# A hand-written plan that takes in the SyncE queue: the last loads of v, the first expert's weights and the end of the attention stage in another order

## The chip, the core and the metric

The kernel runs on one core of a Trainium2 chip. Five engines work side by side, each through its own list of instructions in order: TensorE (PE: matrix products and transposes), VectorE (DVE), ScalarE (ACT), GpSimd (POOL) and SyncE (SP, which here only issues transfers and reads registers). The metric is the device time of one execution in microseconds (us), the median of several.

## The reference, cut to what matters

```python
# q, k, v: (4, 8, 576, 64); 2304 tokens in all, 512 wide
def _attn_ref(q, k, v):                     # factor = 4
    ...                                     # coarse part: q, k, v averaged in fours, full softmax attention,
    out_up = np.repeat(out_d, factor, axis=2)        # each row repeated four times
    mask = np.abs(pos[:, None] - pos[None, :]) < factor
    scores = np.where(mask, scale * q @ k.T, -1e9)   # local part: a band of 7 keys
    return out_up + softmax(scores) @ v

def _moe_ref(x, expert_emb, tau, w1, w2):   # 8 experts, w1 (8, 512, 1024), w2 (8, 1024, 512)
    logits = xn @ en.T / tau                # rows and embeddings normalized
    expert_idx = np.argmax(logits, axis=1)
    gate_w = probs[np.arange(N), expert_idx]
    for e in range(E):
        mask = expert_idx == e
        h = np.maximum(x[mask] @ w1[e], 0.0)
        out[mask] = gate_w[mask, None] * (h @ w2[e])

def _moe2_ref(x, w_in, w_out):              # 512 -> 2048 -> 512, leaky slope 0.01
    h = x @ w_in
    return np.maximum(0.01 * h, h) @ w_out
```

The three are run one after the other. With the reference's inputs the eight experts get 226, 353, 271, 241, 323, 306, 389 and 195 tokens.

## The kernel before

The 2304 tokens are 18 tiles of 128. The first stage takes each tile through the local attention (scores, softmax, product with v), adds the coarse attention of its batch, stores the row in the HBM buffer `x_d`, and finds the token's expert. The second stage goes through the experts, the third through a dense feed-forward layer. Products of the last two stages are taken in three passes of two halves each (`hi`, the rounded number, and `lo`, the remainder), so each weight tile that is loaded is first cast by ACT (`w_hi`, line 879) and then subtracted by DVE (`w_lo`, line 882).

**The plan.** A text, `ORDER`, lists the steps of the first stage and of the first expert by short names, and a table, `todo`, says which function each stands for. Steps are recorded in that order. Under `tc.manual_schedule` the engines named there (PE, DVE, ACT and POOL) get their instructions in the order recorded; SP is not named, and its instructions are placed by the scheduling layer. The names used below, with the tile's or unit's number behind a dot:

- `S`, `SMX`, `SSB`, `SEX`, `SSM`, `SNM`, `LT`, `LTE`, `LV`, `LX`: the local attention of a tile, from the scores (PE) to the copy of the finished rows out of PSUM (`LX`, ACT, line 574). `LTE` is ACT's copy of the transposed weights (line 543), `LV` PE's product with v (lines 559 to 569). `LAD` is SP's store of the rows to `x_d` (line 578).
- `X`, `XE`, `L`, `LG`, `SQ`, `SP`, `RN`, `LD`, `PF`, `LM`, `LE`, `SE`, `PD`, `SC`: the routing, for a tile or for a group of up to three tiles, named by its last (2, 5, 8, 11, 14, 16, 17). `PD` gives each token's place in its expert's list and adds to the counts `acc`; `SC` scatters token and gate into the lists `id_d` (POOL, line 684).
- `vw.g`: the loads of v for 9 strips of 32 tokens each (SP, lines 321 and 325), g from 0 to 7. Each goes into one of two buffers in turn, `vw_113` and `vw_114`; the last, `vw.7`, goes into a third, `vwl`, which `early` opens in memory that the coarse attention has left, and which `Z.0` and `Z.1` fill with zeros (DVE and POOL, line 759). Tiles 15, 16 and 17 read it.
- `CF` and `FE`: a product with ones sums the counts over the partitions, and DVE finds the expert with the most tokens so far and writes its number to `regs`. SP reads it into a register (line 134). It is the first expert, "slot 0". Before, this comes after `PD.11`, so it goes by 12 tiles.
- `WL.u`: SP's loads of unit u of the first expert's weights (lines 140 and 143, 512 KB each; u from 0 to 3) into one of two buffers; `WH.u.i.c` and `WO.u.i.c`: the cast and the remainder of a quarter of it (i is 0 for w1 and 1 for w2).
- `IA`: SP reads the first 192 places of the first expert's list (`tks`, line 792), after the scatters of tiles 0 to 11. `XR`: POOL gathers those rows from `x_d` (line 775, two gathers of 96). `XG`: ACT multiplies them by the gate (line 819). `XT`, `XH`, `XO`: they are transposed and split. `L1.f`, `RL`, `RO`, `L2.f`: the two products for the 192 rows, in 8 steps of 128 hidden columns. This is "block A".
- `IB`, `XB`, `GB`, `BT`, `BH`, `BO`: the same for the first expert's other 220 places, "block B", whose products follow block A. `CA` and `RK` rank all experts by their counts in between; SP then reads seven more registers, lists and weights.

**What SP's transfers wait for.** A built transfer of SP waits, besides its data, for a semaphore that goes round: the eighth transfer before it must have landed. So SP has at most eight under way.

**The fence.** `fence` stores one number of block B's `xhi` to HBM, and is recorded behind the plan; what SP has behind it waits until block B's rows are split.

Of the kernel before, what the change touches and what calls it, by code (L numbers as in the profile page):

```python
# [8 lines left out]
F32 = mybir.dt.float32  # L9
# [7 lines left out]
EngineType = mybir.EngineType  # L17
# [3 lines left out]
B, H, S, D = 4, 8, 576, 64  # L21
NP = H // 2
# [5 lines left out]
P = 128  # L28
# [5 lines left out]
GS = 9  # L34
NSTRIP = S // STRIP
# [6 lines left out]
CA = 192  # L42
# [14 lines left out]
                 LTE="ACT", XE="ACT", dE="ACT", LX="ACT"))  # L57
# [27 lines left out]
dx.3.0 LV.9 LAD.7 RN.8 LTE.10 SSB.12 E.3.0.1.1 SEX.12 dT.3.0.0 LD.8 LX.9 LT.11 dE.3.0.0 LV.10 LAD.9 SSM.12 P.3.0.1  # L85
SQ.9 LTE.11 LM.8 S.14 LE.8 LX.10 SE.8 PF.8 SNM.12 X.9 LAD.10 SQ.10 SMX.14 ds.3.1 PD.8 XE.9 SSB.14 dT.3.0.1 SC.8 dm.3.1
LT.12 SEX.14 LV.11 vw.6 dE.3.0.1 SSM.14 LTE.12 db.3.1 X.10 LX.11 dv.3.0 XE.10 SNM.14 X.11 SQ.11 do.3.0 L.9 dx.3.1
SP.11 S.13 XE.11 RN.11 dT.3.1.0 LG.9 SMX.13 dh.3.0 L.11 dE.3.1.0 SSB.13 dT.3.1.1 LAD.11 dl.3.0 LG.11 dT.3.1.2 SEX.13
L.10 dE.3.1.1 SSM.13 S.15 dE.3.1.2 SNM.13 LG.10 dv.3.1 LD.11 SMX.15 LT.13 LM.11 SSB.15 LE.11 PF.11 LV.12 do.3.1 SEX.15
LTE.13 PD.11 dh.3.1 CF LT.14 LX.12 SQ.12 LTE.14 dl.3.1 LV.13 LX.13 FE early WL.0 SE.11 LV.14 S.16 LX.14 SQ.13 Z.1  # L90
SC.11 X.12 XE.12 Z.0 LAD.12 X.14 S.17 SMX.16 SSB.16 SEX.16 SSM.16 SNM.16 L.12 SMX.17 SQ.14 XE.14 LG.12 SSM.15 WH.0.0.1
vw.7 WH.0.1.1 X.13 WL.1 SSB.17 XM XE.13 WO.0.1.1 LT.16 SEX.17 L.14 IA SSM.17 LTE.16 LG.14 LAD.13 L.13 WH.0.1.0 LG.13
SNM.15 LT.15 LTE.15 WH.0.0.0 CS LD.14 SP.14 SNM.17 RN.14 XR LM.14 LE.14 FC SE.14 LV.16 PF.14 LT.17 LX.16 X.16 LV.15
LTE.17 PD.14 WH.1.0.0 WO.1.0.0 WH.1.0.1 WO.1.0.1 WO.0.1.0 XE.16 LX.15 SQ.15 LAD.14 WO.0.0.0 WO.0.0.1 X.15 XE.15
WH.1.1.1 WO.1.1.1 SQ.16 L.16 LG.16 L.15 LV.17 SC.14 LG.15 LD.16 PF.16 SP.16 RN.16 LM.16 WH.1.1.0 PD.16 XG XT.0 LX.17
X.17 LE.16 SQ.17 SE.16 SP.17 XH.0 SC.16 XE.17 XO.0 WO.1.1.0 XT.1 XH.1 XO.1 WL.2 XT.2 WL.3 XH.2 XO.2 L.17 LG.17 LD.17
XT.3 XH.3 XO.3 RN.17 LM.17 PF.17 PD.17 LE.17 cut LAD.15 L1.0 WH.2.0.0 L1.2 WH.2.1.0 SE.17 SC.17 RL.0 LAD.17 RO.0 L1.3
RL.3 WH.3.1.0 LAD.16 L2.0 RO.3 RL.2 L1.1 CA WH.3.0.0 WH.3.0.1 WH.2.1.1 L2.3 WH.2.0.1 RO.2 RL.1 WO.2.0.0 WO.3.0.1
WO.3.1.0 WO.3.0.0 L2.2 WH.3.1.1 RO.1 L2.1 RK IB WO.2.0.1 XB WO.2.1.1 WO.2.1.0 L1.7 RL.7 RO.7 WO.3.1.1 GB L1.5 RL.5
L2.7 RO.5 BT.0 BH.0 BO.0 BT.1 BH.1 BT.2 BT.3 BH.3 BO.1 BO.3 L1.4 L2.5 L1.6 RL.4 RO.4 L2.4 BH.2 RL.6 RO.6 BO.2 L2.6  # L100
"""
# [9 lines left out]
def tile_kernel(ctx, tc, q, k, v, emb, tau, w1, w2, win, wout, out):  # L111
    nc = tc.nc
    V, A, G, T = nc.vector, nc.scalar, nc.gpsimd, nc.tensor
# [46 lines left out]

    man = tc.manual_schedule(engines={EngineType.PE, EngineType.DVE, EngineType.Activation, EngineType.Pool})
    st1 = ExitStack()
    with man:
# [125 lines left out]
        raw, qT, kT, qd, kd, vw, vd = ({} for _ in range(7))  # L289
# [842 lines left out]
        def w_half_lo(u, i, c):  # L1132
# [194 lines left out]
```

## Time and profile before

| | us |
|---|---|
| median of 3 runs (lowest, highest) | 839.29 (835.18, 843.37) |
| the profiled execution: its time | 839.96 |
| its span | 838.0 |
| TensorE busy | 801.2 |
| VectorE busy | 473.6 |
| ScalarE busy | 337.4 |
| GpSimd busy | 213.9 |

A profile is taken of one execution, and its times count from the start of the span; 1.96 us of the execution's time lie around the span. Busy time is a sum over instructions; that of TensorE is modelled from its pipeline, so a busy TensorE is not one at its peak. The granted clock is a share of full speed: 1.00 is 2.4 GHz and 0.50 is 1.2 GHz.

### The profile page before, as it was taken

Reading aid. Unit: us, or ns where it says so; the run is one execution under the profiler, and the core shown is the slowest. Engines: PE = TensorE matmul, PEld = TensorE weight load, DVE = VectorE, ACT = ScalarE, POOL = GpSimd, SP = SyncE. Lnnn points to the kernel's source line nnn. Section 1 sums busy time; section 2 is a strip of 40 time slices with the busy share of each in tenths; the row PEclk is TensorE's granted clock in tenths of the full one; section 3 lists DMA queues with packets and bytes.
Section 4 is the critical chain, followed back from the end, with each engine's and each line's share of the span. In section 5 each row is a group of like instructions: output and inputs, shape, how many; then the busy total and the mean of one; then the engine's idle time right before and its main releaser. Section 6 shows DMA issues by size and latency. Waiting matters only on the chain. (4 is left out here: it accounts for less than half of the span.)

```text
span 838.0 us, 17581 instructions
## 1 busy us (share of the span) xinstructions
PE 801.2 (96%) x7150; PEld 726.3 (87%) x7150; DVE 473.6 (57%) x920; ACT 337.4 (40%) x686; POOL 213.9 (26%) x246
## 2 busy tenths in 40 slices
PE   7999998689999999999998999999999999999995
PEld 6777876489999999999987889999999999999994
DVE  7657877453778897896589972332322332232222
ACT  3564675442555455565433322332222222222221
POOL 8466664332213324431033410100001001001001
PEclk9999999779999999999999999999999999999999
DMA  9999746627477688776554300111011011001001
GB/s 273 159 208 193 166 120 122 196 86 163 153 248 219 204 261 254 236 239 220 166 162 140 102 24 1 38 40 37 0 39 38 1 38 39 0 1 38 1 1 40
DMA packets 104646, 97.78 MB, mean 117 GB/s; under 512 B 58956, under 2 KB 83148, under 8 KB 104562
## 3 DMA queue, kind: packets, MB, share of 16 engines
q1 hardware_dynamic: 94018, 69.88, 31.2%
q0 software_dynamic: 10544, 26.74, 10.3%
q8 instruction: 58, 0.95, 0.5%
q14 instruction: 26, 0.21, 0.1%
HBM read 81.48 MB, written 15.12 MB: 115 GB/s over the span
## 5 line engine op out<-in xcount | busy, mean ns | idle before, releaser
L936 PE MATMUL psh<-xhi,w 128*128 128x384 f32 (+9 forms) x672 | 216.2, 322 | 0.3 <-DVE xlo L831 0.3
L937 PE MATMUL psh<-xlo,w 128*128 128x384 f32 (+9 forms) x672 | 215.8, 321 | 0.0
L938 PE MATMUL psh<-xhi,w 128*128 128x384 f32 (+9 forms) x672 | 215.4, 321 | 0.0
L968 DVE SCALAR_TENSOR_TENSOR hs<-hs 128x384 f32<-128x384 f32 x96 | 62.0, 645 | 186.1 <-ACT hs L967 186.1
L936 PEld LDWEIGHTS psh<-xhi,w 128*128 128x128 f32 x672 | 127.9, 190 | 4.4 <-DVE xlo L831 0.5
L937 PEld LDWEIGHTS psh<-xlo,w 128*128 128x128 f32 x672 | 127.9, 190 | 3.9
L938 PEld LDWEIGHTS psh<-xhi,w 128*128 128x128 f32 x672 | 127.8, 190 | 0.0
L967 ACT COPY hs<-psh 128x384 f32<-128x384 f32 x96 | 46.0, 479 | 194.3 <-PE psh L938 190.8
L1021 PE MATMUL pso<-w,hh 128*128 128x512 f32 x282 | 112.9, 400 | 3.8 <-ACT hh L973 3.1
L1022 PE MATMUL pso<-w,hh 128*128 128x512 f32 x282 | 110.9, 393 | 0.0
L1052 POOL DMA_INDIRECT out_dram<-o,tk x18 | 17.9, 993 | 320.9 <-ACT o L1051 315.4
L973 ACT CAST hh<-hs 128x384 fp32r<-128x384 f32 x94 | 48.2, 513 | 93.7 <-DVE hs L968 93.7
L882 DVE TENSOR_TENSOR w<-r,w 128x1024 fp32r<-128x1024 f32 (+1 forms) x72 | 82.3, 1153 | 5.0 <-ACT w L879 4.0
L1009 PE MATMUL psy<-hh,w 128*128 128x192 f32 (+8 forms) x288 | 81.2, 304 | 0.0
L1019 PE MATMUL pso<-w,hl 128*128 128x512 f32 x282 | 80.9, 394 | 0.0
L924 POOL TENSOR_TENSOR ds<-r 128x512 f32<-128x512 f32 x32 | 42.5, 1328 | 146.7 <-DVE r L922 56.4
L1010 PE MATMUL psy<-hh,w 128*128 128x192 f32 (+8 forms) x288 | 78.9, 296 | 0.0
L974 DVE TENSOR_TENSOR hl<-hs,hh 128x384 fp32r<-128x384 f32 x94 | 52.4, 557 | 45.9 <-ACT hh L973 45.9
L988 ACT ACTIVATE hh<-psh 128x192 fp32r<-128x192 f32 (+8 forms) x72 | 29.2, 406 | 110.8 <-PE psh L938 110.3
L879 ACT CAST w<-r 128x1024 fp32r<-128x1024 f32 (+1 forms) x72 | 67.7, 947 | 5.7 <-DMA r<-in_moe_w_dram 5.7
L1021 PEld LDWEIGHTS pso<-w,hh 128*128 128x128 f32 x282 | 52.9, 188 | 17.2 <-ACT hh L973 8.2
L1019 PEld LDWEIGHTS pso<-w,hl 128*128 128x128 f32 x282 | 53.0, 188 | 12.9 <-DVE hl L974 0.3
(232 smaller groups left out, 1234.7 us busy)
## 6 DMA issues: line engine op xcount, KB each, us to landing
r<-in_moe_w_dram SPq DMA_DIRECT2D x64, 512.0 KB
r<-in_moe_w_in_dram POOLq DMA_DIRECT2D x16, 512.0 KB, 4.1
r<-in_moe_w_out_dram POOLq DMA_DIRECT2D x16, 512.0 KB, 4.1
vw<-in_v_dram SPq DMA_DIRECT2D x56, 96.0 KB
vg<-in_v_dram SPq DMA_DIRECT2D x8, 576.0 KB
x_d<-xt SPq DMA_DIRECT2D x18, 256.0 KB
yc<-yT_d SPq DMA_DIRECT2D x6, 768.0 KB
qk<-in_q_dram SPq DMA_DIRECT2D x4, 576.0 KB
```

The source lines that it names most:

```text
L879: A.copy(w[:, 0, i, cs], src)
L882: V.tensor_tensor(out=w[:, 1, i, cs], in0=src, in1=w[:, 0, i, cs].bitcast(F32), op=ALU.subtract)
L936: T.matmul(ps, lh, rh, start=start, stop=False)
L937: T.matmul(ps, lh, rl, start=False, stop=False)
L938: T.matmul(ps, ll, rh, start=False, stop=stop)
L968: V.scalar_tensor_tensor(out=hs, in0=hs, scalar=0.01, in1=hs, op0=ALU.mult, op1=ALU.max)
L974: V.tensor_tensor(out=gl[:, 0:n], in0=hs, in1=gh[:, 0:n].bitcast(F32), op=ALU.subtract)
L1009: T.matmul(ps, wh, hh[:, 0:n], start=f == 0, stop=False, skip_group_check=True)
L1010: T.matmul(ps, wl, hh[:, 0:n], start=False, stop=False, skip_group_check=True)
L1019: T.matmul(ps, hl[:, c], wh, start=False, stop=f == NF2 - 1, skip_group_check=True)
L1021: T.matmul(ps, hh[:, c], wh, start=f == 0, stop=False, skip_group_check=True)
L1022: T.matmul(ps, hh[:, c], wl, start=False, stop=False, skip_group_check=True)
```

## The change

SP is named in `tc.manual_schedule`, so that its instructions too stand in the order recorded. The fence goes. `CF` and `FE` move up behind `PD.8`, so the first expert is chosen by nine tiles' counts (with these inputs that is expert 6 with 257 tokens of 1152, and by 12 tiles it is expert 6 with 304 of 1536). The third buffer and its zeros go; `vw.7` takes `vw_114`, whose last reader before it is `LV.13`. The rest of the plan from there to block B is written in another order. Of the table the diff shows the lines around `CF`.

```diff
-SQ.9 LTE.11 LM.8 S.14 LE.8 LX.10 SE.8 PF.8 SNM.12 X.9 LAD.10 SQ.10 SMX.14 ds.3.1 PD.8 XE.9 SSB.14 dT.3.0.1 SC.8 dm.3.1
...
-LTE.13 PD.11 dh.3.1 CF LT.14 LX.12 SQ.12 LTE.14 dl.3.1 LV.13 LX.13 FE early WL.0 SE.11 LV.14 S.16 LX.14 SQ.13 Z.1
...
+SQ.9 LTE.11 LM.8 S.14 LE.8 LX.10 SE.8 PF.8 SNM.12 X.9 LAD.10 SQ.10 SMX.14 ds.3.1 PD.8 CF FE XE.9 SSB.14 dT.3.0.1 SC.8
+dm.3.1 LT.12 SEX.14 LV.11 vw.6 WL.0 WL.1 dE.3.0.1 SSM.14 LTE.12 db.3.1 X.10 LX.11 dv.3.0 XE.10 SNM.14 X.11 SQ.11
...
+LV.12 do.3.1 SEX.15 LTE.13 dh.3.1 dl.3.1 early WH.0.0.0 WH.1.1.0 WH.1.0.0 PD.11 WO.0.0.0 SE.11 SC.11 LX.12 LT.14
...
-    man = tc.manual_schedule(engines={EngineType.PE, EngineType.DVE, EngineType.Activation, EngineType.Pool})
+    man = tc.manual_schedule(engines={EngineType.PE, EngineType.DVE, EngineType.Activation, EngineType.Pool, EngineType.SP})
...
-            t = vwt[g] = vws[-1 if g == B * NSTRIP // GS - 1 else len(vwt) % O['NVW']]
+            t = vwt[g] = vws[len(vwt) % O['NVW']]
...
-            vws.append(stv.enter_context(tc.tile_pool(name="pv", bufs=1)).tile([P, NP, GS, 2, D], F32, name="vwl"))
-
-        def zeros(i):
-            (V, G)[i].memset(vws[-1][:, 2 * i:2 * i + 2], 0.0)
...
-            stv.close()
...
-        fence_d = dram.tile([1, 1], F32, name="fence_d")
-
-        def fence():
-            nc.sync.dma_start(out=fence_d, in_=xTs["e", 0][0].bitcast(F32)[0:1, 0, CA:CA + 1])
...
-        at(-1.0, fence)
```

On SP, from the last piece of `vw.6` to the first expert's list (`tks`), the kernel before has (`r_2832` and `r_3009` are units 0 and 1 of the weights):

```order
L325 DMA vw_113<-in_v_dram 48x4x64
L578 DMA x_d<-xt 128x512
L134 TENSOR_LOAD regs
...
L140 DMA r_2832<-in_moe_w_dram 128x4x256
...
L143 DMA r_2832<-in_moe_w_dram 128x2x512
...
L321 DMA vwl<-in_v_dram 48x8x64 x4
...
L140 DMA r_3009<-in_moe_w_dram 128x4x256
...
L143 DMA r_3009<-in_moe_w_dram 128x2x512
...
L792 DMA tks<-id_d 96x2x2
```

and the changed one (its lines are numbered one or some higher or lower; `r_2486` and `r_2489` are units 0 and 1):

```order
L326 DMA vw_113<-in_v_dram 48x4x64
L135 TENSOR_LOAD regs
...
L141 DMA r_2486<-in_moe_w_dram 128x4x256
...
L144 DMA r_2486<-in_moe_w_dram 128x2x512
...
L141 DMA r_2489<-in_moe_w_dram 128x4x256
...
L144 DMA r_2489<-in_moe_w_dram 128x2x512
L579 DMA x_d<-xt 128x512 x2
L322 DMA vw_114<-in_v_dram 48x8x64 x4
...
L788 DMA tks<-id_d 96x2x2
```

Both units of weights have moved ahead of the stores of tiles 11 and 12 and of `vw.7`, and nothing but `vw.7` stands between those stores and the list.

On ACT, from the copy `LTE.13` (the first row) to the copies of tiles 13 and 14, before:

```order
L543 COPY leT<-psLT 128x512
L468 CAST dnh<-dnt 128x384
L574 COPY xt<-psLV 128x4x2x64
L586 ACTIVATE junk,ss<-xt 128x512
L543 COPY leT<-psLT 128x512
L574 COPY xt<-psLV 128x4x2x64 x2
```

and in the changed kernel, where line 875 is the cast of a quarter of the weights (`WH`):

```order
L544 COPY leT<-psLT 128x512
L469 CAST dnh<-dnt 128x384
L875 CAST w<-r_2486 128x512
L875 CAST w<-r_2489 128x512 x2
L575 COPY xt<-psLV 128x4x2x64
L544 COPY leT<-psLT 128x512
L875 CAST w<-r_2489 128x512
L575 COPY xt<-psLV 128x4x2x64
```

Three casts, two of them of unit 1 and the first of these of its second transfer, now stand ahead of `LX.12` and `LTE.14`.

On PE, from the transposes of the gathered rows (`xe`) to the first product of block A (`psh`), before:

```order
L156 MATMUL psx<-ident,xe 128x96 x2
L156 MATMUL psX<-ident,xt 128x128 x4
L156 MATMUL psx<-ident,xe 128x96 x4
L613 MATMUL psL<-enT,xT 64x8 x8
...
L660 MATMUL psR<-oh,tri 128x8
...
L936 MATMUL psh<-xhi,w 128x192
```

and in the changed kernel:

```order
L157 MATMUL psX<-ident,xt 128x128 x4
L157 MATMUL psx<-ident,xe 128x96 x4
...
L157 MATMUL psx<-ident,xe 128x96 x2
L614 MATMUL psL<-enT,xT 64x8 x8
...
L932 MATMUL psh<-xhi,w 128x192
...
L661 MATMUL psR<-oh,tri 128x16
...
L1005 MATMUL psy<-hh,w 128x192
```

The routing of tile 17 and the ranks of the groups 16 and 17 (`PF.16`, `L.17`, `PF.17`) have moved behind the first products of block A. In block B the four transposes `BT`, which stood among block A's last products, now stand behind them all.

## Rows read from the trace of the kernel before

**Rows 1.** The page: its first line.

```profile
span 838.0 us, 17581 instructions
```

**Rows 2.** Windows: busy us (count) of PE, PEld, DVE, ACT, POOL; clock, DMA, GB/s.

```profile
136.50:173.80 37.30, 25.50 (x435) 18.80 (x433) 20.61 (x72) 19.17 (x48) 15.54 (x17) 0.76 0.66 173
...
173.80:199.70 25.90, 25.61 (x203) 25.26 (x204) 12.64 (x43) 8.80 (x22) 8.57 (x7) 0.89 0.46 131
...
199.70:838.00 638.30, 624.84 (x3638) 579.67 (x3637) 343.11 (x579) 232.80 (x445) 105.46 (x99) 1.00 0.32 100
```

**Rows 3.** Two-microsecond stretches, the same columns.

```profile
128.00:130.00 2.00, 1.29 (x63) 1.10 (x55) 1.72 (x7) 0.37 (x2) 0.24 (x1) 1.00 0.80 128
...
142.00:144.00 2.00, 1.39 (x22) 0.98 (x20) 1.93 (x5) 0.82 (x3) 1.58 (x2) 1.00 1.30 282
...
144.00:146.00 2.00, 0.57 (x16) 0.48 (x14) 1.15 (x3) 1.48 (x4) 1.53 (x2) 0.91 1.34 95
...
146.00:148.00 2.00, 2.00 (x20) 1.91 (x19) 1.64 (x6) 1.32 (x5) 0.69 (x1) 0.50 0.62 94
...
154.00:156.00 2.00, 2.00 (x19) 1.33 (x21) 0.98 (x4) 1.94 (x4) 0.00 (x0) 0.53 0.93 323
...
164.00:166.00 2.00, 0.00 (x0) 0.00 (x0) 0.00 (x0) 0.00 (x0) 1.70 (x2) 1.00 0.29 77
...
174.00:176.00 2.00, 2.00 (x10) 2.00 (x11) 1.51 (x11) 1.32 (x3) 0.00 (x0) 0.50 0.79 280
```

**Rows 4.** Timeline of SP: start us, us, what it issues.

```profile
120.18 4.14 SPq L321 DMA_DIRECT2D vw<-in_v_dram  x4
...
126.91 0.47 SPq L325 DMA_DIRECT2D vw<-in_v_dram  x1
...
137.71 0.42 SPq L140 DMA_DIRECT2D r<-in_moe_w_dram  x1
...
152.49 0.34 SPq L792 DMA_DIRECT2D tks<-id_d  x1
...
171.56 0.37 SPq L140 DMA_DIRECT2D r<-in_moe_w_dram  x1
...
179.85 0.33 SPq L792 DMA_DIRECT2D tks<-id_d  x1
...
206.95 0.24 SPq L1117 DMA_DIRECT2D fence_d<-xhi  x1
...
217.17 0.41 SPq L140 DMA_DIRECT2D r<-in_moe_w_dram  x1
```

**Rows 5.** Timeline of the other engines, in brackets the idle time before.

```profile
133.60 0.59 ACT L574 COPY xt<-psLV 128x512 f32<-128x512 f32 x1 [0.69 <-PE psLV L569]
...
133.96 2.02 POOL L759 MEMSET vwl<- 128x2304 f32 x1 [5.71 <-DVE ckey L706]
...
136.44 0.15 DVE L721 CAST regs<-ca 128x1 int32<-128x1 f32 x1
...
137.52 1.98 DVE L759 MEMSET vwl<- 128x2304 f32 x1 [0.43 <-issue]
...
144.52 0.62 ACT L879 CAST w<-r 128x512 fp32r<-128x512 f32 x1 [1.70 <-DMA r<-in_moe_w_dram]
...
159.72 1.30 POOL L775 DMA_INDIRECT xe<-x_d,tks  x1 [11.93 <-DMA x_d<-xt]
...
166.43 0.72 ACT L819 ACTIVATE xe<-xe,tks 96x512 f32<-96x512 f32 x1 [5.83 <-issue]
...
167.20 0.42 PE L156 MATMUL psx<-ident,xe 96*128 96x96 f32 x1 [5.03 <-ACT xe L819]
...
173.79 0.51 PE L936 MATMUL psh<-xhi,w 128*128 128x192 f32 x1
...
182.53 1.12 POOL L775 DMA_INDIRECT xb<-x_d,tks  x1 [5.51 <-PE psy L1007]
...
199.74 0.29 PE L936 MATMUL psh<-xhi,w 128*128 128x220 f32 x1
```

More of the change, by code (lines that the diff above doesn't have):

```diff
@@ L85 @@
 dx.3.0 LV.9 LAD.7 RN.8 LTE.10 SSB.12 E.3.0.1.1 SEX.12 dT.3.0.0 LD.8 LX.9 LT.11 dE.3.0.0 LV.10 LAD.9 SSM.12 P.3.0.1
-SQ.9 LTE.11 LM.8 S.14 LE.8 LX.10 SE.8 PF.8 SNM.12 X.9 LAD.10 SQ.10 SMX.14 ds.3.1 PD.8 XE.9 SSB.14 dT.3.0.1 SC.8 dm.3.1
-LT.12 SEX.14 LV.11 vw.6 dE.3.0.1 SSM.14 LTE.12 db.3.1 X.10 LX.11 dv.3.0 XE.10 SNM.14 X.11 SQ.11 do.3.0 L.9 dx.3.1
-SP.11 S.13 XE.11 RN.11 dT.3.1.0 LG.9 SMX.13 dh.3.0 L.11 dE.3.1.0 SSB.13 dT.3.1.1 LAD.11 dl.3.0 LG.11 dT.3.1.2 SEX.13
-L.10 dE.3.1.1 SSM.13 S.15 dE.3.1.2 SNM.13 LG.10 dv.3.1 LD.11 SMX.15 LT.13 LM.11 SSB.15 LE.11 PF.11 LV.12 do.3.1 SEX.15
@@ L90 @@
-LTE.13 PD.11 dh.3.1 CF LT.14 LX.12 SQ.12 LTE.14 dl.3.1 LV.13 LX.13 FE early WL.0 SE.11 LV.14 S.16 LX.14 SQ.13 Z.1
[L91 to L99, printed above, removed]
@@ L100 @@
-L2.7 RO.5 BT.0 BH.0 BO.0 BT.1 BH.1 BT.2 BT.3 BH.3 BO.1 BO.3 L1.4 L2.5 L1.6 RL.4 RO.4 L2.4 BH.2 RL.6 RO.6 BO.2 L2.6
+SQ.9 LTE.11 LM.8 S.14 LE.8 LX.10 SE.8 PF.8 SNM.12 X.9 LAD.10 SQ.10 SMX.14 ds.3.1 PD.8 CF FE XE.9 SSB.14 dT.3.0.1 SC.8
+dm.3.1 LT.12 SEX.14 LV.11 vw.6 WL.0 WL.1 dE.3.0.1 SSM.14 LTE.12 db.3.1 X.10 LX.11 dv.3.0 XE.10 SNM.14 X.11 SQ.11
+do.3.0 L.9 dx.3.1 SP.11 S.13 XE.11 RN.11 dT.3.1.0 LG.9 SMX.13 dh.3.0 L.11 dE.3.1.0 SSB.13 dT.3.1.1 LAD.11 dl.3.0 LG.11
+dT.3.1.2 SEX.13 L.10 dE.3.1.1 SSM.13 S.15 dE.3.1.2 SNM.13 LG.10 dv.3.1 LD.11 SMX.15 LT.13 LM.11 SSB.15 LE.11 PF.11
@@ new lines @@
+LV.12 do.3.1 SEX.15 LTE.13 dh.3.1 dl.3.1 early WH.0.0.0 WH.1.1.0 WH.1.0.0 PD.11 WO.0.0.0 SE.11 SC.11 LX.12 LT.14
+LAD.12 SSM.15 LTE.14 LV.13 WH.1.1.1 LX.13 XM WH.1.0.1 LV.14 LX.14 S.17 X.14 vw.7 WH.0.1.0 SQ.12 S.16 SMX.17 SSB.17
+X.13 SQ.13 SEX.17 XE.14 WO.1.0.1 SSM.17 WO.1.1.1 XE.13 L.14 SNM.15 WO.1.0.0 L.13 LG.14 LT.15 SNM.17 LTE.15 LG.13
+SMX.16 SSB.16 SEX.16 SSM.16 CS X.12 XE.12 IA FC LT.17 L.12 LG.12 LD.14 WO.1.1.0 SNM.16 LT.16 SQ.14 SP.14 LAD.13 RN.14
+PF.14 PD.14 WH.0.1.1 LV.15 XR LTE.16 WH.0.0.1 LTE.17 LM.14 LV.16 LE.14 SE.14 LX.15 SQ.15 WO.0.1.0 SC.14 LX.16 SQ.16
@@ new lines @@
+SP.16 LV.17 XG WO.0.0.1 X.16 XE.16 WO.0.1.1 XT.0 LAD.14 XT.1 XH.0 XO.0 XH.1 XO.1 LX.17 WL.2 X.15 RN.16 XE.15 LAD.17
+cut XT.2 XH.2 XO.2 L.16 LG.16 XT.3 XH.3 XO.3 LAD.16 L.15 LG.15 LD.16 LM.16 X.17 LE.16 LAD.15 SQ.17 L1.0 RL.0 SE.16
+PF.16 XE.17 L1.1 SP.17 PD.16 RL.1 L.17 SC.16 RO.0 L2.0 LG.17 RN.17 WH.2.1.1 WH.2.0.1 LD.17 L1.3 PF.17 LM.17 LE.17
+WH.2.0.0 SE.17 RO.1 L2.1 PD.17 RL.3 WL.3 WH.3.1.1 L1.2 RL.2 RO.3 L2.3 WO.2.0.0 WO.2.0.1 L1.5 WH.3.0.0 WO.3.0.0
+WH.3.0.1 WO.3.0.1 L1.7 RL.5 RO.5 L1.4 SC.17 WH.3.1.0 WO.3.1.1 WO.3.1.0 IB XB RO.2 CA WO.2.1.1 L2.2 WH.2.1.0 WO.2.1.0
@@ L101 @@
+L2.5 RK RL.4 RO.4 L1.6 RL.6 L2.4 RL.7 RO.6 L2.6 RO.7 L2.7 GB BT.0 BT.1 BH.0 BO.0 BT.2 BT.3 BH.1 BO.1 BH.2 BH.3 BO.2
+BO.3
 """
@@ L167, in tile_kernel @@
         pl = st.enter_context(tc.tile_pool(name="pl", bufs=2))
-        stq, stv = ExitStack(), ExitStack()
+        stq = ExitStack()
         pd = stq.enter_context(tc.tile_pool(name="pd", bufs=2))
@@ L1144, in tile_kernel @@
             SE=(rt_se,), PD=(rt_pos,), SC=(rt_scatter,), fill=(fill_ids,), K=(consts_k,), CF=(count_pe,
-            "first"), FE=(first_expert,), CS=(count_pe, "snap"), FC=(first_count,), early=(early,), Z=(zeros,),
+            "first"), FE=(first_expert,), CS=(count_pe, "snap"), FC=(first_count,), early=(early,),
             WL=(w_moe_load, 0), WH=(w_half_hi,), WO=(w_half_lo,), IA=(x_ids, "A"), XM=(a_rows,),
```

## The prediction

> **What bounds the kernel now.** I read the windows of the whole span of 838.0 us [rows 1] first, ten microseconds each, and cut the span at the places where TensorE's busy time or its clock changes. Behind 199.70 us the span is TensorE's alone: 624.8 of 638.3 us busy at clock 1.00 [rows 2]. Nothing that only moves work of other engines there can show in the time. The stretch to look at is 136.5 to 173.8: PE is busy 25.5 of 37.3 us, at a mean clock of 0.76, and no other engine is busy for more than 20.6 of it [rows 2]. So it is a chain of waits. Then I followed the timeline back from the first product of block A, at 173.79 [rows 5]. It needs the transposes of the gathered rows, at 167.20, which had 5.03 us of idle time before them and waited for ACT's gate; ACT got the first rows at 166.43; POOL sent the gather at 159.72 after 11.93 us of idle time [rows 5]. The gather needs the first expert's list, which SP asked for at 152.49 [rows 4], 7.2 us before. The same request at 179.85 was answered by a gather at 182.53, 2.7 us later [rows 4, 5]. In the slow case unit 1 of the weights had been sent just ahead of it, behind `vw.7`. The profile names a store to `x_d` as what the gather waited for; the store that it needs, of tile 11, was long out, and the list is what came last. So the gate is the place of the list in SP's queue. At 164 to 166 PE did nothing, and at 174 to 176, in block A, it still ran at 0.50 [rows 3].
>
> **The change part by part.** Times are on the clock of the profiled execution.
>
> *FE moved up.* Six DVE operations of about 0.15 us (the last of them is a row [rows 5]) with gaps, some 1.1 us, and one small product that PE waits for, now stand between `PD.8` and tile 14's scores, before `LV.11` and so before `vw.6`. Bounds are 0 (all hidden) and 2 us; I take 0.6, since PE has other work there except for the wait of the one product. Behind `PD.11` as much goes, under PE's work.
>
> *The third buffer.* Fills of 2.02 us on POOL and 1.98 on DVE go [rows 5]. In the kernel before the DVE fill ended at 139.5, and `vw.7` went out just behind it. Now `vw.7` waits for the store of tile 12 instead, which comes out at 139.3 (below). So the fills are worth nothing by themselves.
>
> *The weights first.* SP is through with `vw.6` at 126.91 + 0.47 = 127.4 [rows 4], with FE's 0.6 at 128.0. Reading the register takes 1.1 (from 136.44 + 0.15, the write, to 137.71, the next issue [rows 4, 5]), so `WL.0` goes at 129.1 in place of 137.71, with `WL.1` behind it: four transfers of 0.524 MB, 2.1 MB. The small pieces of v still move up to 130, at 128 GB/s [rows 3]. The weights alone moved at 280 GB/s at 174 to 176, behind the issue at 171.56 [rows 3, 4]; 2.1 MB / 280 = 7.5 us, so the last lands at 137.5. Bounds: 136.5 by the 323 GB/s of 154 to 156, and 146.4 by the 128 of v's pieces [rows 3]; I take 280, the nearest row, with weights and nothing else. The Trainium skill, page "DMA: Bandwidth & Descriptors", section "Anatomy of one DMA — SWDGE (gpsimd) path", gives 2.0 us and the bytes at 436 GB/s for one transfer; by it the four would be there at about 135.9 (an estimate from that page, for a path that SP does not use), and the sum would come out 1.6 us lower. The rows here never show that rate for weights.
>
> *A new wait on ACT.* The first cast of unit 1 needs the last of these four transfers and stands ahead of `LX.12` and `LTE.14`. ACT waits from about 134 to 137.5; two casts at 0.62 [rows 5] then put `LX.12` at 138.7. It ran at 133.60 [rows 5], so it is 5.1 us late. Behind it in the queue are `LTE.14`, all later copies and the store of tile 12; PE waits for `LX.12` with `LV.14`, which needs the PSUM buffer, and has nothing else from about 136.5 on. This is what the change pays.
>
> *Work left.* From `LV.14` to the first product, PE has 25.5 us at 0.76, or 19.4 us at full clock [rows 2]. `L.17`, `PF.16` and `PF.17`, about 1 us by their share of these pieces, move behind it. PE starts on the 18.4 us at 139.2, so block A can't begin before 157.6. ACT has 19.17 us in that stretch [rows 2], of which some 2 us moves ahead of `LX.12` or behind block A's start, so it ends near 156. Both are floors.
>
> *The list.* The store of tile 12 leaves SP at 139.3, then `vw.7`. The ten transfers of `vw.6` took from 120.18 to 127.38 [rows 4]; twelve at this pace take 8.6, so the list is asked for at 148.0. No weights stand ahead of it, so I take 2.7 for its answer (bounds 2.7 and 7.2, the two cases above): gather at 150.7. From the gather to the first transpose it took 7.5 (159.72 to 167.20 [rows 5]) while unit 2 of the weights was moving too; that unit now stands behind the gate, so I take 6.0 (bounds 3.5, half of it, and 7.5): 156.7. From there to the first product it took 6.6 at clock 0.50 [rows 3, 5]; with as much work at full clock, but four copies of ACT between, I take 5.3. Block A begins at 162.0 in place of 173.79.
>
> *Block A to block B.* It took 199.74 − 173.79 = 25.95 us [rows 5] at a mean clock of 0.89 [rows 2], which is 23.1 us of work at full clock. Added are the 1 us of routing and 0.7 for `BT`, whose copies now have no other products beside them (four copies and subtractions, the first of which nothing covers). That is 24.8 us, and block B begins at 186.8 if the clock is full, 2.9 later if it is as low as before.
>
> *The fence and the register reads.* The fence left at 206.95, and the next weights only at 217.17 [rows 4], when a buffer came free, so it costs nothing now. Of the reads, each 1.1 us on SP, one now stands before each expert's stores; PE's work hides them. Uncovered they would be 8 times 1.1. I take 0 for both.
>
> **The sum.** 199.74 − 186.8 = 12.9 us come off. Against the profiled execution that is 839.96 − 12.9 = 827.0; this execution is 0.7 over the median of the three runs, so 826.4 to 827. I forecast 827, with a range of its own of 822 to 832.
>
> **Rivals.**
>
> *The clock falls in the new wait (835).* Before, the clock was 0.91 in 144 to 146 and 0.50 from then on, after 142 to 146, in which PE was busy 1.96 of 4 us; it was still 0.53 at 154 to 156 [rows 3]. The new wait on ACT leaves PE idle for more than 2 us near 137. If that lowers the clock for as long, some 10 us, PE loses 5 us of its floor, block A begins near 167, and if it runs at the low clock too, block B begins at 167 + 24.8 + 2.9 = 194.7: 5.1 us come off, 834.9. Against it: 128 to 130 had 0.7 us idle and stayed at 1.00 [rows 3], and the loss overlaps with the wait for the list. The Trainium skill, page "TensorE: Matmul & The Clock Gate", section "What's actually happening", has the low clock as the state of rest, out of which activity brings the engine; by that rule this case is the one to expect, and the trace agrees for 142 to 146.
>
> *The weights come sooner (822).* At 323 GB/s or more, with the list and the rows at their lower bounds, only PE's floor stays: 157.6 + 24.8 = 182.4, 17.3 us off, 822.6.
>
> *The weights come too late (844), slower than before.* Their 2.1 MB share the queue with v's small pieces ahead and the store of tile 11 behind, and ACT, and with it all of the stage, stands until the last of them is there. Before, unit 0 was sent at 137.71, and ACT had its second half only at 144.52 [rows 4, 5], with v's pieces moving. At 128 GB/s the last lands at 146.4, 8.9 later than I take, block A begins at 162.0 + 8.9 + 5 (the low clock) = 175.9, and block B at 175.9 + 24.8 + 2.9 = 203.6: 3.8 slower. With the low clock it is slower from a landing past 142.6 on, that is, under 170 GB/s.
>
> *It doesn't do what it says (838).* Nine tiles could name another expert; by the counts they don't, and both the capacity of 412 and the later ranking stay as they were. Or the gather waits for something else that does not move, and only a microsecond or two comes off.
>
> **How the numbers follow.** Chances: the forecast 0.50, the low clock 0.28, sooner 0.10, too late 0.08, nothing moved 0.04. The range of 820 to 837 takes in the first three and leaves out the other two. About 1%, 8.4 us, is what a measurement of this kernel can tell from no change. Faster by more than that (under 830.9): most of the forecast's 0.50 (0.44), all of sooner, a little of the low clock, 0.58. Slower by more: a part of too late, 0.03. Within 1%: 0.39.
>
> **What would show it.** In the changed profile: weights at about 129 on SP; a cast of ACT with 3 to 4 us of idle time before it, ended by a weight transfer, near 137; the list at about 148 and the gather 3 us behind it; the first product of block A near 162, at clock 1.00; the first of block B near 187; and from there to the end 638 us as before. I am wrong if the cast does not wait, if the list is answered as slowly as before, or if the gain up to block B is lost behind it.

## The result, and the profile after

The changed kernel takes 833.31 us (median of 13 runs, 830.06 to 836.61), the kernel before 842.77 beside it (13 runs, 835.18 to 844.68). The ratio of the two means (833.52 and 841.44) is 0.9906, with a 95% interval of 0.9879 to 0.9933: some 7.9 us come off. I had forecast 827.0 from a profiled execution of 839.96, 12.9 us off, with a range of 820 to 837. So the sign and the range held, and about five of the thirteen microseconds did not come.

The profiled execution after took 833.75 us. The page's first line and the windows of it (the columns of [rows 2]):

```profile
span 831.8 us, 17573 instructions
...
139.80:167.50 27.70, 22.38 (x415) 17.22 (x415) 13.17 (x46) 18.68 (x46) 12.03 (x13) 0.82 0.55 133
167.18:191.02 23.84, 23.55 (x225) 23.19 (x223) 14.42 (x60) 9.88 (x27) 8.42 (x8) 1.00 0.44 133
191.02:831.80 640.78, 625.95 (x3636) 580.04 (x3636) 344.00 (x582) 232.62 (x447) 108.83 (x102) 1.00 0.32 101
```

The stretch ahead of block A is shorter and at a higher clock (0.82 against 0.76), and block A to block B now takes 23.84 us at 1.00, against 25.95 at 0.89 [rows 2]. But from block B's first product to the end it is 640.78 us in place of 638.26: 2.5 us are given back there. Stretches of two microseconds show where TensorE stands still (same columns):

```profile
140.00:142.00 2.00, 0.00 (x0) 0.00 (x0) 0.00 (x0) 0.49 (x1) 1.70 (x2) 0.93 0.19 54
142.00:144.00 2.00, 0.81 (x2) 0.50 (x2) 0.00 (x0) 2.00 (x5) 1.80 (x3) 0.50 0.01 1
...
156.00:158.00 2.00, 2.00 (x24) 1.28 (x26) 1.63 (x10) 1.07 (x2) 1.43 (x3) 0.50 0.21 63
...
202.00:204.00 2.00, 0.65 (x3) 0.28 (x2) 0.00 (x0) 1.80 (x3) 0.00 (x0) 1.00 0.30 79
```

The first two are the new wait on ACT, with the clock at 0.50 behind it; at 156 to 158 the clock is low again; the last one lies in block B, where nothing waited before. SP's timeline, beside [rows 4]:

```profile
130.86 0.91 SPq L141 DMA_DIRECT2D r<-in_moe_w_dram  x1
...
143.59 1.98 SPq L322 DMA_DIRECT2D vw<-in_v_dram  x4
...
151.41 0.33 SPq L788 DMA_DIRECT2D tks<-id_d  x1
...
185.47 0.32 SPq L788 DMA_DIRECT2D tks<-id_d  x1
186.12 0.41 SPq L141 DMA_DIRECT2D r<-in_moe_w_dram  x1
```

And the other engines, beside [rows 5], with the idle time ahead in brackets:

```profile
141.51 1.14 ACT L875 CAST w<-r 128x512 fp32r<-128x512 f32 x2 [5.56 <-DMA r<-in_moe_w_dram]
142.56 0.58 ACT L575 COPY xt<-psLV 128x512 f32<-128x512 f32 x1
...
155.31 0.88 POOL L591 TENSOR_TENSOR ss<-ss,half_c 128x3 f32<-128x3 f32 x1 [0.29 <-ACT junk L587]
156.45 1.09 POOL L771 DMA_INDIRECT xe<-x_d,tks  x1 [0.26 <-POOL ss L591]
...
163.44 0.72 ACT L815 ACTIVATE xe<-xe,tks 96x512 f32<-96x512 f32 x1 [0.56 <-DMA xe<-x_d,tks]
...
167.18 0.34 PE L932 MATMUL psh<-xhi,w 128*128 128x192 f32 x1
...
191.02 0.37 PE L932 MATMUL psh<-xhi,w 128*128 128x220 f32 x1 [0.29 <-DVE xlo L827]
...
202.20 1.95 ACT L815 ACTIVATE xe<-xe,tks 124x512 f32<-124x512 f32 x3 [2.49 <-DMA xe<-x_d,tks]
```

What the prediction named is there: the cast of unit 1 waits for the weights and holds `LX.12` (L575); the gather no longer has weights ahead of its list. New is the wait on the last row, for the gathered rows of expert 1.

### The profile page after: what moved, and what is told of

It reads as the page before. It is cut to its first block, busy times and chain, and to the rows that moved or that the text cites. A ratio compares the mean times of both kernels' runs of the same rounds, so it can differ in the third digit from the quotient of the medians.

```text
span 831.8 us, 17573 instructions
## 1 busy us (share of the span) xinstructions
PE 797.5 (96%) x7150; PEld 723.4 (87%) x7150; DVE 466.9 (56%) x919; ACT 336.3 (40%) x686; POOL 212.9 (26%) x245
## 5 line engine op out<-in xcount | busy, mean ns | idle before, releaser
L932 PEld LDWEIGHTS psh<-xhi,w 128*128 128x128 f32 x672 | 126.5, 188 | 4.7 <-DVE xlo L827 0.5
L934 PEld LDWEIGHTS psh<-xhi,w 128*128 128x128 f32 x672 | 126.6, 188 | 0.0
L875 ACT CAST w<-r 128x1024 fp32r<-128x1024 f32 (+1 forms) x72 | 67.8, 947 | 10.4 <-DMA r<-in_moe_w_dram 10.4
L1015 PEld LDWEIGHTS pso<-w,hl 128*128 128x128 f32 x282 | 52.9, 188 | 12.9 <-DVE hl L970 0.3
```

The source lines that it names most:

```text
L875: A.copy(w[:, 0, i, cs], src)
L932: T.matmul(ps, lh, rh, start=start, stop=False)
L934: T.matmul(ps, ll, rh, start=False, stop=stop)
L1015: T.matmul(ps, hl[:, c], wh, start=False, stop=f == NF2 - 1, skip_group_check=True)
```

## The experiments

Twelve kernels, in three sets of four. Each set ran on one chip, and the ratios are to the kernel before on that chip. The chips differ: the kernel before took 846.59, 841.89 and 845.66 us on the three. So ratios are compared within a set, and traces by three distances: from the copy of tile 11 (`LX.11` on ACT) to block A's first product; from there to block B's; and from there to the end. Of the change only the early choice (`FE`) lies ahead of `LX.11`; its 1.5 us (below) are not in these distances. In microseconds, from each kernel's one profiled execution:

| kernel | `LX.11` | to block A | to block B | to the end |
|---|---|---|---|---|
| before | 120.92 | 52.87 | 25.95 | 638.26 |
| changed (the result) | 123.81 | 43.37 | 23.84 | 640.78 |
| changed, second set | 121.86 | 43.64 | 23.84 | 640.66 |
| casts behind | 127.58 | 44.96 | 23.84 | 641.02 |
| rows first | 128.25 | 46.62 | 29.22 | 644.51 |
| gather ahead | 129.34 | 45.90 | 23.83 | 640.93 |
| plan only | 128.16 | 49.29 | 29.79 | 637.86 |
| filled wait | 121.71 | 45.30 | 23.84 | 640.95 |
| list ahead | 120.77 | 50.25 | 34.37 | 638.41 |
| early choice | 124.48 | 43.74 | 30.13 | 637.85 |
| ranking early | 122.23 | 45.38 | 30.25 | 639.94 |
| weights held | 129.98 | 45.33 | 23.84 | 638.85 |
| both | 124.08 | 45.62 | 23.84 | 639.06 |
| plan undone | 123.75 | 45.80 | 23.83 | 644.12 |

**First set.** *The casts moved behind* (of the changed kernel's ORDER):

```
-early WH.0.0.0 WH.1.1.0 WH.1.0.0 PD.11 WO.0.0.0 SE.11 SC.11 LX.12 ... LTE.14 LV.13 WH.1.1.1 LX.13 XM
+early PD.11 SE.11 SC.11 LX.12 ... LTE.14 LV.13 WH.1.1.1 LX.13 WH.0.0.0 WH.1.1.0 WH.1.0.0 WO.0.0.0 XM
```

> The changed kernel with the first three casts of unit 1 and the remainder of unit 0 (WH.0.0.0 WH.1.1.0 WH.1.0.0 WO.0.0.0) moved in ORDER from behind `early` to behind LX.13. Theory (the weights' landing is the gate of the stage): LX.12 no longer stands behind the wait of 5.56 us, runs near 137 in place of 142.56, the store of tile 12 and the list come some 5 us earlier, PE has no idle time at 140 to 142, and block A begins near 163 in place of 167.18; about 829 us against 833.3. Rival (the work behind is the gate: POOL's queue ahead of the gather and the casts, which now come later, take as long): LX.12 comes earlier, block A stays at 167 and the time at 833 within 1.5. A second rival: the casts now fall into the copies of tiles 14 to 17 and block A comes later, 835 or more.

0.9986 (0.9955 to 1.0017). In its trace (its lines are numbered one lower):

```profile
138.83 0.58 ACT L574 COPY xt<-psLV 128x512 f32<-128x512 f32 x1 [0.69 <-PE psLV L569]
...
145.55 0.62 ACT L874 CAST w<-r 128x512 fp32r<-128x512 f32 x1 [5.58 <-DMA x_d<-xt]
146.08 0.58 ACT L574 COPY xt<-psLV 128x512 f32<-128x512 f32 x1
...
160.27 1.09 POOL L770 DMA_INDIRECT xe<-x_d,tks  x1 [0.26 <-POOL ss L590]
```

`LX.12` runs 11.3 us behind `LX.11` in place of 18.8, and `vw.7` goes out 6 us sooner; but one cast of unit 1 (WH.1.1.1) was still ahead of `LX.13` and waits there as long (the profile names a store to `x_d`, but what the cast reads is weights, sent up to 138.35). I had overlooked it, so the edit takes the wait from one tile, not from the stage. Even so it tells something: the gather goes 32.7 us behind `LX.11`, as in the changed kernel (32.6), right behind POOL's power of tile 14. Block A comes no sooner behind `LX.11`.

*Expert 1's gathers ahead of its weights in the plan*:

```
-at(-0.6, x_rows, 1)
+at(-0.85, x_rows, 1)
```

> The changed kernel with the gathers of expert 1's rows put ahead of both of its first weight units in the plan (before them stand only its list). Theory: PE's idle time at 202 to 204, 1.6 to 2 us, comes from the gathered rows that share the queues with 2.1 MB of weights sent just ahead of them; with the rows ahead, the transposes of expert 1 don't wait, the way from block B's first product to the end is 638.5 in place of 640.8, and the time is 1.5 to 2.3 lower, 831 to 832. Rival: the list of expert 1 (its six small pieces) is what is late, since the gathers wait 4.80 us for it; then the gathers land no earlier and the time stays at 833.3, or the weights, now behind the wait, make the casts of expert 1's units late and the time goes up by a microsecond or two.

0.9971 (0.9945 to 0.9997). The edit does nothing to the order that counts: the gathers are POOL's and the weights SP's, and while POOL waits 5.40 us for the list, SP sends the weights. ACT still waits 3.19 for the rows:

```profile
201.41 1.40 POOL L771 DMA_INDIRECT xe<-x_d,tks  x1 [5.40 <-DMA tks<-id_d]
...
215.97 1.95 ACT L815 ACTIVATE xe<-xe,tks 124x512 f32<-124x512 f32 x3 [3.19 <-DMA xe<-x_d,tks]
```

*The gather ahead of POOL's power of tile 14*: `SQ.14 XR SP.14` in place of `SQ.14 SP.14 ... XR`.

> The changed kernel with the gather of block A's rows (XR) ahead of POOL's power of tile 14 (SP.14). Theory: the list was there by 154 and POOL's queue held the gather (the power at 155.31 waits for ACT's squares at 154.50); the gather goes at 154.3 to 154.6 in place of 156.45, but ACT's gate stands right behind the squares of tile 16, at 162, so block A gains 0 to 1 us: 832.3 to 833.3. Rival (the list itself came at 156): the gather stays at 156.4, waits for the list, the power and all of tile 14's routing behind it come 1 to 2 us later, and the time is 833 to 834.

0.9968 (0.9936 to 1.0000). The gather goes 3.65 us behind the list (157.95 to 161.60) in place of 5.04 (4.43 in the second execution of the changed kernel), so POOL's queue had held it for about a microsecond. Even so 3.65 is not the 2.7 of my sum. ACT's gate runs at 169.05 with no idle time ahead, behind the squares of tile 16, and block A comes no sooner: no gain, as the theory had it.

*The kernel before with SP in the plan and no fence*:

```
-man = tc.manual_schedule(engines={..., EngineType.Pool})
+man = tc.manual_schedule(engines={..., EngineType.Pool, EngineType.SP})
-        at(-1.0, fence)
```

> The kernel before with two parts of the change alone: SP in the plan's order, and no fence store. Theory of the prediction (the fence and the register reads cost nothing): 0, that is 842 within 1, block A at 173 to 174, 638 us from block B to the end. Rival: a part of the gain comes from here, since SP no longer sends transfers by its own priorities and no store waits for block A's transposes: 1 to 3 us less, 839 to 841, with the weights of expert 1 and the list of block B sent earlier.

1.0041 (1.0009 to 1.0074): no gain, and rather a small loss. From block B to the end it takes as long as before. But from block A to block B the trace has 3.8 us more, and the low clock at block A's start doesn't explain them, since the kernel before has it too [rows 3]. SP asks for block B's list 10.0 us behind block A's first product, where it was 6.1 [rows 4, 5]; the rows then meet both of expert 1's first weight units (sent from 192.59 to 194.51), and PE, which has their transposes among block A's products, waits:

```profile
187.45 0.34 SPq L792 DMA_DIRECT2D tks<-id_d  x1
...
197.66 0.88 PE L156 MATMUL psx<-ident,xb 110*128 110x110 f32 x7 [2.30 <-DVE xb L817]
...
200.00:202.00 2.00, 2.00 (x11) 0.50 1.16 286
```

The last row is a window of PE alone (busy, clock, DMA, GB/s): the clock fell behind this wait. So in the old order SP's place in the plan can cost something, where I had taken 0; in the new one the transposes stand behind all of block A's products. Why the list is asked for later was not tried.

The three variants of the changed kernel stood at 0.9968 to 0.9986 on this chip, and not one of their intervals reaches down to that of the changed kernel (0.9879 to 0.9933). It itself did not run there. So either the edits cost something or the gain is smaller on this chip; that stays open, and the set says little on times.

**Second set.** *The changed kernel as it is*, as the measure.

> The changed kernel as it is, on the chip of the runs beside it, as the measure for them. Theory (the gain belongs to the change): the same ratio as at first, 0.9906 within its interval of 0.988 to 0.993. Rival (a large part of it hangs on how the front stage, which no part of the change touches, and the granted clock in the last stretch fall out on a chip): the ratio is nearer to 1, 0.994 to 0.998, as in the three variants of the first set, and block A's first product comes 4 to 8 us later than 167.18 with a lower clock around it.

0.9907 (0.9885 to 0.9929), the first result again. Its profiled execution, 831.99 us with a span of 830.0, is the better one to check the prediction on, since tile 14's scores, ahead of every part of the change, start at 115.01 here (116.62 in the one above), close to the kernel before:

```profile
128.35 0.42 SPq L141 DMA_DIRECT2D r<-in_moe_w_dram  x1
...
138.96 1.14 ACT L875 CAST w<-r 128x512 fp32r<-128x512 f32 x2 [4.50 <-DMA r<-in_moe_w_dram]
...
150.08 0.33 SPq L788 DMA_DIRECT2D tks<-id_d  x1
...
154.51 1.09 POOL L771 DMA_INDIRECT xe<-x_d,tks  x1 [0.26 <-DMA x_d<-xt]
...
161.63 0.25 PE L157 MATMUL psx<-ident,xe 96*128 96x96 f32 x1
...
165.50 0.34 PE L932 MATMUL psh<-xhi,w 128*128 128x192 f32 x1
...
189.34 0.37 PE L932 MATMUL psh<-xhi,w 128*128 128x220 f32 x1 [0.29 <-DVE xlo L827]
```

Block B starts 10.4 us sooner than before, 2.4 are lost behind it, and 8.0 stay: the ratio's 7.8.

*The wait filled*: `LT.14+24` in place of `LT.14`, 24 products that nothing uses.

> The changed kernel with 24 spare products (128x256, bf16, into the PSUM buffer of tile 14's transposes, ahead of them) which TensorE runs while ACT waits for the weights; nothing else changes. Theory (the clock falls because of the idle time in that wait, and costs): the clock stays at 1.00 in the 8 us behind the wait, where it was 0.50 to 0.86; the 6.8 us of PE's work there shrink by some 2 us, and block A comes 1 to 3 us earlier against the changed kernel beside it. Rival (the stretch is gated by ACT and POOL, and PE has room at either clock): the clock rises and block A stays where it is, within 1 us. If the clock falls all the same, the idle time was not its cause.

0.9913 (0.9883 to 0.9944). Windows of PE alone (busy, clock, DMA, GB/s):

```profile
142.00:144.00 2.00, 1.47 (x93) 1.00 0.25 90
144.00:146.00 2.00, 0.84 (x11) 1.00 0.75 118
146.00:148.00 2.00, 2.00 (x71) 0.50 0.42 89
...
156.00:158.00 2.00, 2.00 (x30) 0.50 0.51 178
```

The clock stays at 1.00 through the wait, falls at 146, behind a stretch in which PE was busy 0.84 of 2 us, and stays at 0.50 until 158. Block A comes 1.7 later behind `LX.11` than without. So in this execution filling the wait moved the fall of the clock to the next gap, and nothing was gained.

*The list of block A ahead of unit 1's weights, in the kernel before*: `IA ... XR WL.1` in place of `WL.1 ... IA ... XR`, on top of the plan's parts.

> The kernel before with SP in the plan and no fence (as in the run with the plan's parts alone), and unit 1 of the weights (WL.1) moved behind the gather's step XR, so that the list of block A (IA) stands ahead of it in SP's queue. Theory of the prediction (the list's place behind the weights is the gate): the gather comes 3 us behind the list in place of 6 to 7, block A 3 to 5 us earlier than in the run with the plan's parts alone, ratio to before 0.998 or less against 1.0041. Rival (the store of tile 11 or POOL's queue holds the gather): the gather stays 6 us behind the list, ratio 1.004. Second rival: unit 1 comes too late for its casts, and block A's products wait for them in place of the rows.

1.0088 (1.0057 to 1.0118), slower. The first half of the theory holds: list at 150.67, gather at 153.52, 2.85 us behind it where it was 7.2, and block A starts at 171.02, 2.8 sooner than [rows 5]. That is little: the gather goes 6.2 sooner than before, and as early behind `LX.11` (32.8) as in the changed kernel, but block A comes 6.9 later than there. What stands in its place is the second rival. Unit 1 now leaves at 152.75, and its first casts hold a copy of rows on ACT, which PE needs for the routing ahead of block A:

```profile
157.39 1.14 ACT L879 CAST w<-r 128x512 fp32r<-128x512 f32 x2 [3.21 <-DMA r<-in_moe_w_dram]
...
159.55 0.77 PE L156 MATMUL psX<-ident,xt 128*128 128x128 f32 x3 [2.75 <-ACT xt L574]
```

Between block A and block B 8.4 us are lost:

```profile
186.32 1.08 POOL L775 DMA_INDIRECT xb<-x_d,tks  x1 [0.31 <-PE psh L938]
186.37 0.41 SPq L140 DMA_DIRECT2D r<-in_moe_w_dram  x1
...
194.88 0.49 DVE L817 TENSOR_SCALAR xb<-xb,tks 110x512 f32<-110x512 f32 x1 [7.37 <-DMA xb<-x_d,tks]
...
195.42 0.81 PE L156 MATMUL psx<-ident,xb 110*128 110x110 f32 x3 [5.25 <-DVE xb L817]
```

Block B's second gather goes out together with 2.1 MB of expert 1's weights and takes 8 us. In the old order `BT` stands among block A's products, so PE waits 5.25 us with products of block A behind it. The run with the plan's parts alone has the same wait, 2.30 us, so it does not come from the list's new place alone.

*The early choice alone* (CF FE behind PD.8, WL.0 WL.1 behind vw.6; casts, third buffer and last stretch as before), again with the plan's parts:

> The kernel before with SP in the plan and no fence, and of the rest of the change only the early choice: CF FE behind PD.8, WL.0 WL.1 right behind vw.6. The casts, the third buffer and the last stretch stay in the order of before. Theory: with all weights there before 142, the casts of before (from about 142 on) don't wait, the list has no weights ahead of it, and block A comes 4 to 7 us earlier than with the plan's parts alone: ratio 0.995 to 0.999, most of what the whole change brings. Rival (the gain is in the new order of the last stretch, which keeps TensorE at its clock before block A): the list is answered sooner, but the ratio stays above 1.001.

0.9954 (0.9926 to 0.9983): half of the gain. Block A comes as early behind `LX.11` as in the whole change, and 5.6 us earlier than with the plan's parts alone. The list is asked for at 153.02 and answered by the gather at 155.70, 2.7 us. But block A to block B takes 6.3 more than in the new order:

```profile
173.47 0.62 ACT L879 CAST w<-r 128x512 fp32r<-128x512 f32 x1 [2.81 <-DMA r<-in_moe_w_dram]
```

The casts of the next units wait for their weights (2.81 us here and 2.93 at 177.47), which leave SP at 161.23 and 166.83. PE is idle for 4.9 us of this stretch, 1.1 of them for a row of block B, and some 4 us of it ran at a clock of 0.55 to 0.59 (from 190.22 on).

**Third set.** *Ranking early*: CA behind L1.2, RK behind WO.3.0.1.

> The changed kernel with the last count (CA) moved up behind L1.2 and the ranking of the experts (RK) behind WO.3.0.1, so that expert 1 is known some 4 us earlier (regs near 180.5 in place of 184.25). Theory (what block B gives back behind its start is expert 1's rows, which are asked for too late): list of expert 1 near 181.7 in place of 185.47, its gathers near 184.5 in place of 188.34, no idle time of PE at 202 to 204, the way from block B's first product to the end 638.5 in place of 640.8; ratio 0.9907 - 0.0024 = 0.988. Rival (the 2.1 MB of expert 1's weights, which come forward with the list, now meet block B's own rows, as in the run with the list ahead): block B's rows land late, block B itself starts 1 to 4 us later, ratio 0.991 to 0.995.

0.9917 (0.9887 to 0.9947): no gain, the rival. PE's windows, the wait for block B's rows, and the issues of that stretch (count, median us to landing):

```profile
160.00:162.00 2.00, 0.00 (x0) 1.00 0.90 282
...
166.00:168.00 2.00, 2.00 (x22) 0.50 1.44 296
```

```profile
196.16 0.49 DVE L813 TENSOR_SCALAR xb<-xb,tks 110x512 f32<-110x512 f32 x1 [2.87 <-DMA xb<-x_d,tks]
```

```profile
xb<-x_d,tks POOLq DMA_INDIRECT x2, 6.5
```

Expert 1's weights now meet block B's rows, which take 6.5 us (3.9 in the changed kernel). Most of the 30.25 us from block A to block B is something else, though: PE waited 3.2 us for block A's gathered rows (159.7 to 162.9), and ran at 0.50 from 166 to 178, the first products of block A among it. The theory's first half holds: expert 1's rows are asked for earlier, ACT doesn't wait for them, and from block B to the end it is 639.94, 0.7 to 0.8 less than in the changed kernel.

*Expert 1's weights held until its rows are there* (a word of the third gather's rows stored in between):

```
+        def hold():
+            nc.sync.dma_start(out=held_d, in_=rows[1][2][0:1, 0:1])
-        at(-0.8, w_moe_load, 1, 0)
-        at(-0.7, w_moe_load, 1, 1)
-        at(-0.6, x_rows, 1)
+        at(-0.8, x_rows, 1)
+        at(-0.7, hold)
+        at(-0.6, w_moe_load, 1, 0)
+        at(-0.5, w_moe_load, 1, 1)
```

> The changed kernel with expert 1's weights held on SP until its gathered rows have landed (one store of a word of the third gather's rows stands between). Theory (the weights sent just ahead of the gathers take the transfer engines from them): the rows land in 3 to 5 us in place of up to 13.8, before 197, and PE doesn't wait for their transposes; 1.5 to 2.3 us off, ratio 0.988 to 0.989, unless the weights now land behind 204, where the first cast of expert 1 stands. Rival (a gather takes that long by itself, since each of its packets is a row of its own): the rows land no earlier than 199, PE's idle time stays, and the weights come late on top: ratio 0.991 to 0.995.

0.9872 (0.9838 to 0.9905). The gathers' time to landing, here and in the changed kernel:

```profile
xe<-x_d,tks POOLq DMA_INDIRECT x3, 7.0
```

```profile
xe<-x_d,tks POOLq DMA_INDIRECT x3, 12.5
```

ACT's gate on them (207.73) has no idle time ahead, PE stands nowhere in block B, and 1.8 to 1.9 us of the way to the end are gone. The first cast of expert 1 waits 1.30 us for its weights, and nobody waits for that.

*Both of these edits.*

> Both of the last two edits: ranking early, weights held until expert 1's rows are there. Theory: rows asked for at 184.5 and there by 190, weights sent at 190 to 192 and there by 200, nothing waits behind block B's start: 638.3 from there to the end, the lowest time of all, ratio 0.987 to 0.989. If ranking early alone is as good, the weights' place doesn't matter once the list is early; if holding alone is as good, the list's time doesn't matter.

0.9875 (0.9840 to 0.9911). The word is stored at 198.57, 5.0 us behind block B's start, where it was 8.5; nothing waits, and nothing more is gained.

*The plan and the fence undone in the changed kernel.*

> The changed kernel with its first two parts undone: SP no longer in the plan's order, so the scheduler places SP's transfers, and the fence store back. Theory of the prediction (both cost nothing and bring nothing): ratio 0.9907 within 0.001. Rival (with SP in the plan expert 1's second weight unit is sent right behind the first, ahead of its rows, and that is what costs the 2 us behind block B): with SP free the rows of expert 1 don't wait, 638.3 from block B to the end, ratio 0.988. Second rival: the scheduler puts the store of tile 12 among the pieces of `vw.7`, the list comes later, ratio 0.992 or more.

0.9901 (0.9868 to 0.9934), the changed kernel's ratio. The rows of expert 1 take 13.4 us here too, and ACT waits 3.15 us for them, so it isn't SP's place in the plan that sends the weights ahead of them; that rival falls. The 644.12 us to the end, 3.3 more than in the changed kernel, show what the same wait can cost: behind it the clock fell, to 0.50 from about 207 to 213 (PE alone).

```profile
204.00:206.00 2.00, 0.37 (x5) 1.00 0.50 122
...
208.00:210.00 2.00, 2.00 (x11) 0.50 0.04 8
```

The run with the gathers first has the same: 0.50 behind the wait, and 644.51. In the five other executions with late rows the clock stayed at 1.00.

The two kernels with the hold are the fastest of all, 0.987 of before. The changed kernel did not run on their chip, and the intervals overlap with its 0.9907; on the same chip and with nothing but the hold between them, the kernel with both edits takes 834.57 and the one with the early ranking alone 838.08, though only part of these 3.5 us lies behind block B (639.06 and 639.94).

## Why the prediction was right, and where it was off

**The gate was the first expert's late weights: shown. That it was the list's place alone: not.** With the early choice alone block A comes 9.1 us sooner behind `LX.11` than before (52.87 to 43.74; 5.6 against the plan's parts alone), and the whole change adds nothing to that. But the early choice does two things: no weights stand ahead of the list, and units 0 and 1 are there when ACT casts them. The list ahead does the first alone, and block A comes 2.6 sooner (50.25); there the casts of unit 1 wait in the list's place. So the wait for the list was the last one, as I had read it, but right behind it stood another that the early weights take away too, which I had not named. Without weights ahead the list is answered in 2.7 and 2.85 us in the old order of the last stretch, the value I took.

**The terms**, in the execution whose front agrees with that of before: first weights 128.35 (I said 129.1), the cast's wait ended 138.96 (137.5), list 150.08 (148.0), gather 154.51 (150.7), first transpose 161.63 (156.7), block A 165.50 (162.0), block B 189.34 (186.8). Against my sum the errors up to block A add up to 3.5 us: 1.5 for the cast, 0.6 for the list behind it, 1.7 for its answer, 1.1 from the gather to the transposes, less 1.4 from there to the first product (3.9 us in place of 5.3), which is luck. Block A to block B takes back another 1.0, so half of the five microseconds that did not come are lost ahead of block B and half behind it. FE costs 1.5 us, not 0.6: tile 14's scores start 0.5 sooner than before and their subtraction on DVE 1.0 later. It is inside my bounds. The weights come 1.5 later than I took (10.6 us from the first issue to the cast). The two figures of the Trainium skill, page "DMA: Bandwidth & Descriptors", section "Anatomy of one DMA — SWDGE (gpsimd) path", had given about 135.9, an estimate from that page for a path that SP does not use; the trace does not agree (138.96), and the measurement decides.

**The step that failed ahead of block A** is the list's answer and what follows: 4.4 and 7.1 us in place of 2.7 and 6.0 (5.0 and 7.1 in the first execution). I had made the list the only chain. There are two, the list with its gather and the work of tiles 14 to 17 on PE, ACT and POOL, and they end together: the power of tile 14 stands ahead of the gather on POOL, and the squares of tile 16 ahead of the gate on ACT. This fits that moving the gather forward and filling the wait brought nothing by themselves.

**Block A to block B** was 24.8 in my sum and is 23.84. The 0.7 that I had put on `BT` behind the products did not come: PE is idle for 0.3 us of the whole stretch (23.55 busy), as it was before, and at full clock. In the old order the kernels with the plan's parts alone, with the list ahead and with the early choice take 29.79, 34.37 and 30.13, and in all three a late row of block B stops block A's products (2.30, 5.25 and 1.10 us). Which part of the new order does most of this was not tried.

**Behind block B** I took 638 us as before. It is 640.7, the largest single error (2.4): I had carried the stretch over as it was, without asking what an earlier block B collides with. Before, its first product came 8.6 us behind expert 1's first gather; now 2.7. The gather before and after, and the time to landing before:

```profile
191.12 1.40 POOL L775 DMA_INDIRECT xe<-x_d,tks  x1 [5.65 <-PE psh L938]
```

```profile
188.34 1.40 POOL L771 DMA_INDIRECT xe<-x_d,tks  x1 [4.80 <-DMA tks<-id_d]
```

```profile
xe<-x_d,tks POOLq DMA_INDIRECT x3, 8.2
```

The rows are now also longer under way, 12.5 us in place of 8.2: both weight units leave just ahead of them, where before one did and the second followed at 194.06. So they are late for transposes that stand at a fixed place in block B. With the weights held they take 7.0 and the loss is gone but for 0.6 to 0.8 us, which I can't place.

**The rivals.** The low clock came true in its first half: 0.50 for some 6 us behind the wait. Its second half, a block A at low clock, did not in these two executions (1.00), but did in the runs with the gathers first (0.80 over that stretch) and with ranking early. The measured 833.3 is nearer to that rival's 834.9 than to the forecast's 827, and block A's 167.18 in the first execution is its 167, though by another way; the range held because it took in both. The weights were not too late, and the change did what it says. The fence and the reads, which I had put at 0: undone in the changed kernel, they leave its ratio as it was (0.9901 and 0.9907), but put alone into the kernel before they cost 0.4% (0.1 to 0.7%), of which the trace shows the late rows of block B. The third buffer was not tried by itself.

## What to carry to other kernels

When a gate is taken away, follow the time saved down the rest of the span: a transfer that was in time behind the gate can now be late. An order between two queues (a gather on one, loads on another) isn't set by their places in a plan; what holds is a wait that one of them really has. Before moving a transfer forward, check what it will meet: here the early ranking sent expert 1's weights into block B's rows. And when one wait is taken away, look for the next one behind it: with the list ahead, the casts of unit 1 took its place.

## What the runs showed of the hardware

The same gathers of three times 124 rows took 12.2 to 13.7 us to land with 2.1 MB of weights sent just ahead (five executions), and 6.6 and 7.0 without (two).

Executions differ much ahead of the changed parts: `LX.11`, which only FE's 1.5 us can move, ran between 120.8 and 124.5 us in nine profiled executions and between 127.6 and 130.0 in five, and block A came later by about as much.

With the same instructions up to block A, the clock fell in other places in each execution, and block A came 43.4 to 46.6 us behind `LX.11`. A wait of PE can cost more than its length: where the clock fell behind the wait for expert 1's rows, the way from block B to the end was 5.9 and 6.3 us longer than before (two executions); where it stayed at 1.00 it was 2.4 to 2.8 longer (five).
